# Tail blocks of a fused attention and feed-forward kernel: each batch's 64 query rows on half of TensorE's columns

## The chip, the cores and the metric

The kernel runs on one core of one Trainium2 chip. The metric is device microseconds of one execution. Engine names are those of the profile: PE is TensorE's matmul, PEld its weight load, DVE VectorE, ACT ScalarE, POOL GpSimd, SP the queue that issues most of the DMAs.

## The reference

Causal attention mixed with a retrieved memory, then a gated feed-forward layer. B=4 batches, H=8 heads, S=576 positions, D=64; the feed-forward layer has 512 inputs and 1536 hidden units. Cut to what matters:

```python
scores = scale * q @ k.T ; causal mask ; a = exp(scores - max) ; a /= a.sum(-1) + 1e-9
local = a @ v
q_p = where(q > 0, q, exp(q) - 1) + 1
mem_out = (q_p @ M_prev) / (q_p @ z_prev + 1e-6)
x = g * mem_out + (1 - g) * local          # g = sigmoid(beta), per head
xn = x / rms(x) * rms_g                     # x as 2304 rows of 512
out = (silu(xn @ w_gate) * (xn @ w_val)) @ w_out
```

## The kernel before

**Blocks.** The 2304 rows are worked on in 18 blocks of 128 rows. 576 is four and a half times 128, so each batch has four full blocks and 64 rows over. Two batches share one block for these rows: block 10 holds the last 64 rows of batches 0 and 1, block 17 those of batches 2 and 3. These two are the tail blocks. Rows 0 to 63 of a tail block belong to one batch, rows 64 to 127 to the next. Below they are tail 10 and tail 17.

**Precision.** Operands are split into a high and a low f16 part. Scores are the product of a query tile that holds both parts with a key tile, in two products (`t2` = 0, 1); P V takes three (high by high, high by low, low by high), of 65, 64 and 65 columns; the memory part takes two of 65 columns. The 65th column carries the sum that the result is divided by.

**A tail block before.** TensorE's stationary operand is 128 columns wide, one column for each row of the block. A tail block's keys, values and memory differ between its two halves, so each product is made twice with all 128 rows, once for each batch, into two PSUM tiles, and of each result the half of the rows that doesn't belong to the batch is left unread:

- Scores (`tail_scores`, line 624): for each of 8 heads and each batch four key blocks by two products of 128 columns (L635), evacuated by DVE 64 rows at a time (L639), then two products with the block's own keys (L645, evacuated at L648). 18 products a head.
- P V (`tail_pv`, L748 to L750): for each head, each batch and each of five key blocks three products. 30 a head. The two batches accumulate in the PSUM tiles `a0` and `a1`.
- Memory (`mem_mm`, L848): for each group of four heads and each batch eight products. 32 a block, and two such blocks.

Line 608 and lines 731 to 733 are the scores and P V of full blocks. L848 serves both kinds of block. Between a head's scores and its P V stand the evacuation on DVE, the exponential (ACT, L674), a cast (ACT, L190), the low part (DVE, L693) and a transposing DMA into a `PT` tile (SP, L699).

**The feed-forward layer** works on 9 chunks of two blocks: gate and value products of 256 columns (L1109), then the output products of 512 columns (L1183 to L1185). Its products fill the time in which attention waits. Chunk 8, the last, needs tail 17.

**The order of issue.** `ISSUE` (line 72) writes out for each engine the order of its instructions: letters are kinds (`S` scores, `P` P V, `M` memory, `G` gate and value, `D` output products on PE), a number is a count, and `~` picks one out of turn. Each engine works through its list in that order, so a product that waits holds back all that stand behind it. In the order before, a tail's products mostly alternate with `G` products.

**Buffers.** Scores go through two PSUM buffers (`sc`), which a head of a tail needs three times. `a0` and `a1` have one buffer each.

Of the kernel before, what the change touches and what calls it, by code (L numbers as in the profile page):

```python
# [17 lines left out]
ALU = mybir.AluOpType  # L18
# [66 lines left out]
        "GSD3PDPDPDGPGPGPGPGPSGPSGPSGPSGPSGSGSGSG5PGPGPGPGPGPGPGP5D4SDSDSGSGSGSGSGSPGSPGSPGSPGSPGSPGSPGSPGSPGPGPGPG3S2G5"  # L85
        "D3PDPDPDGPGPGS16PGPGPGPGPGPGPG8PGPGPGPGPGPGPS2GP4YPD4MDMDMGMGMGMGMGMS16GMGMGMGMGMGMGMGMG11D6G2S2G9S8G13D6S6PSPS"
        "P5S2P26GPGPGPGPGPGPGPGPGPGPGPGP2S8GPGPGPGPGPGPGPS8GPGPGPGPGP2S2PD6GPGPGPGPGPGPGPGPS16GPGPGPGPGPGPGPGPGPGPGPGPGP"
        "S2GPGPGP2S8P5~5PP~4PP~3PP~2DPP~1S8P~1PDPDPDPDPDPGPGPGS2PGPGPGPGPGPGPGPGPGPGPGPGPG6SGSGSGS5DSDSDS2DSDSDSM16S2GS"
        "G23D3S8D3G2P20P~10PP~9PP~8PP~7PP~6PP~5PP~4PP~3PP~2PP~1P11GPGPGPSGPSGPSGPSGPSGPSGPSGPSG5PGPGPGPGPGPGPGP5DPDPDPDPD"
        "PDPGPGPGPGPGPSGPSGPSGPSGPSGPSGPSGPSG5PGPGPGPGPGPGPGP5DPDPDPDPDPDPGPGPGPGPGPGPGPGPGPGPGPGPG5SGSGSGSGSGSGSGSD6G12"  # L90
        "M8G5MGMGMGMGMGMGMGMD6G9P24G15D5P12DG4SS~5G13PGPGPGPGPGPGPGP5D6G21S10G3D6G14S6M8S6G10D3MDMDMDMGMGMGMGMGS12G19D5P9"
        "S6DGP9G8SGSGSGSGSGSG8SGSGS6D6G13P9G6S2P9S6G5D6G14P18G3MGMGMGMGMYGMGMGMD3GS8D3G4S2P9S6G12SGSGSGSGSGSGSP9GSD6G17SG"
        "SGSGSGSGSGSGSD6S8G12M6P24M2G9P12G3D6G5SGSGSGSGSGSP12GSGSG12D6P12G24D6G13P12G11P12D6G17S2S2~6G7D4S12D2G2P12G7M8G3"
        "S16G12D6GM4GMGMSGMGMS3G14S4~2GS4G4D6P12D2D2~1S2P12S4D2S6G34MGMGMGMGMGMGMGMP12G7D6G6P12G18D3SDSDSDSGSGSP9G3PGPGPG"
        "PGPGPGPGPGPG4SGSGSGSGSGSG2D4MDMDM6P5G10PGPGPGPG4SGSGSGSGSGSG2D4PDPDPGPGPGPGPGPGPG11SGSGSGSGSGSG2D4PDPDPGPGPGPGPG"
        "PSGPSGSGSGSGSGSGSG5PGPGPGPGPGPGPGP2D4SDSDSGSGSGSGSGSPGPGPGPGPGPGPGPGPG11D3SDSDSDGSGSGSGSGSPGPGPGPGPGPGPGPGPG11D4"
# [12 lines left out]
        "EHCAEHCEACOEOHCEACHNfsXksAECHEFACHEsCsAeEqCHAECHEACHAECHvNfXrAECHkAkHECAFEsHCsAECHECAOoOHEACHE2CE2ACHEvEvAvCsHsq"  # L109
        "AEfNEHCrkAHAXHFs2AqNHfrAEXCECHkEAEFHCEAECHEACsHECs3EACeO2CqHEACov~1v4EHCEACAEHCNfEqCHXrEAC2HEAkHkCAHAFHrAHEkE3C2"  # L110
        "EfNEAqEXEFHCAECErHEACHCEAO2HCNfCAqXkECHAECFHrAECHAECHEACHECAHECANfHXkAECHFAECHEACHEACHEACO2HAECHAECHNEAXCHECAHEC"
        "EACHECAHECAHAHNAXHAHAHAO2HAHAHAHAHAHAHAHAHAHAHO"
    ),
    "DVE": (
        ".2.~1.3I3fIJfZIZfIfI3e~6e~15e~25S4IJe~33UJSiS3iS4TUS4i~1ui2uTi~1u2i~1Tui~2ii~1uTiRiRfRfU2RU6ZUA2tZtUtAt~1tAte~7"
        "t2Ue~15o2fS6fS2i2AuAu2i2~1UA2s2eU2ZTUgege2Ue3AeAe~8UZUAiAg2g~6gg~5gg~4sg2g~2g~4UTg5Ux2AiAsUegxZUS4xeUgeS4eig~16x"
        "eiUe4UuxTuZg~16uUAi~1Ai~1xigZXgg~6Ugg~5TU~1gg~4g2g~2g~4g3Uxgg~1g2g~6gg~5gg~4g2g~2g~4g3Agz~5AgUixUxf2UxAXAkUxqAqA"
        "qvqvqxQkrxUx~3qx~3xqx2~3qkx~4qxAqzAQFxAqAf2rvS2kS2MxM~2AMS2M~1FAMLMLAS2AS2Zv2xALA2zqS2VLAzqVzqVzqzS2QzrzkA2LyS2V"
        "MLAyVMAVMyvALAf2yS2MvVqLMXFVqyMSAVqLvyALqSVyqSAVQvAVyMrL2MySMfAXfAykMqLMqSMqyLAqVSFAqVyQVrALASLSA2SALALV2MVM2SfA"
        "fASLXkSLq3AqAqLMQM2FSArALSV3LA2S2ALALSLA2LVMVMVMSfAfAXSkLSq2AqALq2FQMrM2SALAV3SLA2SLSA2LSLV2AVALM2fMfXSkA2LSFALA"  # L120
        "SM3LSAeAqV2LVSA2LS3A2LS3eqVAeqVAeqVe2qLe2QMSvSe~8fMXrfMASM2ASLkASkAS2LSASAFS2LS2ASALVSV4LSA2M2SMoSM2A2SLSLS2A2L"
# [18 lines left out]
def attn_memory_moe_kernel(  # L140
# [484 lines left out]
    def tail_scores(n, h, s, nm, t, w):  # L625
# [915 lines left out]
```

## Time and profile before

| what | value |
|---|---|
| three runs | 623.01, 628.40, 629.44 us; median 628.4 us |
| the profiled execution | 622.36 us, of which the trace spans 620.6 us |
| PE busy | 598.5 us (96%), 6092 instructions |
| PEld busy | 474.6 us (76%) |
| DVE busy | 451.1 us (73%) |
| ACT busy | 396.8 us (64%) |
| POOL busy | 136.6 us (22%) |
| mean granted TensorE clock | 0.995 |

A product's time in the trace runs from its start to its modelled end, and products overlap: one of 65 columns is shown as 193 ns long, though the next can start about 30 ns later. What a product takes of TensorE's time is therefore read as the distance from its start to the next start in a stretch without waits. The timeline merges neighbours of one kind into a row with a count. Such a row's length is the distances between its starts and one full duration at the end.

### The profile page before, as it was taken

To read this page: it belongs to the slowest core of one execution; us is meant where nothing else is said; L and a number is where in the kernel's file an instruction comes from. 1 tells how busy PE (TensorE), PEld (TensorE's weight loads), DVE (VectorE), ACT (ScalarE), POOL (GpSimd) and SP (SyncE) were. 2 spreads that over 40 slices of the span, in tenths; PEclk is the share of its full clock that TensorE was granted. 3 is DMA by queue.
4 is the path that set the end of the run, shared out by engine and by line. 5 is a ranking of instruction groups with operands and counts; after the bars stand their busy time and mean duration, and the time that the engine had idled before them with its cause. 6 is when DMAs were issued, how large, how long until landed. Compare 5 with 4: busy or idle time off the path is not lost. (4 is left out here: it accounts for less than half of the span.)

```text
span 620.6 us, 15845 instructions
## 1 busy us (share of the span) xinstructions
PE 598.5 (96%) x6092; PEld 474.6 (76%) x6092; DVE 451.1 (73%) x1319; ACT 396.8 (64%) x856; POOL 136.6 (22%) x221
## 2 busy tenths in 40 slices
PE   5979999999999999999999999999999999999996
PEld 4868887677876878788888778778787888887774
DVE  3767688999999687776997777797886757853221
ACT  4587677999887667676466766875775644433221
POOL 2240001124323222121213221132221221112111
PEclk9989999999999999999999999999999999999999
DMA  7997336479868796887489379559995543520001
GB/s 264 361 335 295 103 124 202 135 172 229 149 107 164 149 178 116 176 162 125 71 146 167 80 154 188 106 109 161 164 158 108 86 91 72 94 54 18 35 1 35
DMA packets 183787, 87.57 MB, mean 141 GB/s; under 512 B 165792, under 2 KB 165792, under 8 KB 183712
## 3 DMA queue, kind: packets, MB, share of 16 engines
q1 hardware_dynamic: 180640, 81.82, 62.0%
q10 hardware_dynamic: 3072, 4.74, 2.3%
q8 instruction: 48, 0.79, 0.5%
q14 instruction: 27, 0.22, 0.1%
HBM read 37.77 MB, written 4.72 MB: 68 GB/s over the span
## 5 line engine op out<-in xcount | busy, mean ns | idle before, releaser
L1109 PE MATMUL gv<-xT,wgv 128*128 128x256 f16 x2304 | 312.6, 273 | 0.7 <-DMA xT<-x 0.5
L1109 PEld LDWEIGHTS <-wgv 128*128 128x128 f16 x2304 | 220.0, 98 | 38.9 <-issue 1.5
L1148 POOL TENSOR_TENSOR h<-th,h 128x256 f16<-128x256 f32 x88 | 65.8, 748 | 291.1 <-ACT h L1147 283.8
L674 ACT ACTIVATE S<-S,nm 128x256 f32<-128x256 f32 (+3 forms) x112 | 70.8, 639 | 41.0 <-DVE nm L614 28.4
L1127 DVE SCALAR_TENSOR_TENSOR th<-th,gv 128x256 f32<-128x256 f32 x96 | 39.9, 415 | 62.0 <-ACT th L1126 61.7
L608 PE MATMUL sc<-kT,qT 128*128 128x128 f16 x576 | 79.3, 220 | 0.8 <-DVE nm L614 0.5
L693 DVE SCALAR_TENSOR_TENSOR P<-S,P 128x512 f16<-128x512 f32 (+2 forms) x96 | 67.4, 703 | 17.4 <-ACT P L190 16.8
L1126 ACT ACTIVATE th<-gv,wt 128x256 f32<-128x256 f32 x96 | 44.5, 463 | 54.3 <-PE gv L1109 50.1
L614 DVE CUSTOM_DVE_ANT_0 S<-sc,mask,qsc 128x256 f32<-128x256 f32 (+2 forms) x96 | 57.4, 610 | 17.2 <-PE sc L608 16.7
L1184 PE MATMUL out<-wo,h 128*128 128x512 f16 x176 | 66.8, 380 | 0.0
L1183 PE MATMUL out<-wo,h 128*128 128x512 f16 x176 | 66.3, 379 | 0.0
L1185 PE MATMUL out<-wo,h 128*128 128x512 f16 x176 | 66.1, 379 | 0.0
L190 ACT ACTIVATE P<-S 128x512 f16<-128x512 f32 (+2 forms) x96 | 58.0, 605 | 12.7 <-DMA PT<-P 10.7
L1147 ACT CAST h<-th 128x256 f16<-128x256 f32 x88 | 35.1, 399 | 46.5 <-DVE th L1130 39.0
L608 PEld LDWEIGHTS <-qT 128*128 128x128 f16 x576 | 48.3, 98 | 7.3 <-issue 1.8
L1102 PE MATMUL gv<-xT,wgv 128*128 128x256 f32 x192 | 46.9, 395 | 0.8 <-DVE xT L919 0.8
L1130 DVE SCALAR_TENSOR_TENSOR th<-th,wt,gv 128x256 f32<-128x256 f32 x96 | 45.8, 477 | 1.8
L1102 PEld LDWEIGHTS gv<-xT,wgv 128*128 128x128 f32 x192 | 36.6, 197 | 7.7 <-issue 1.9
L731 PE MATMUL loc<-v,PT 128*128 128x65 f16 x288 | 40.9, 193 | 1.0 <-DMA PT<-P 1.0
L733 PE MATMUL loc<-v,PT 128*128 128x65 f16 x288 | 41.2, 193 | 0.0
L732 PE MATMUL loc<-v,PT 128*128 128x64 f16 x288 | 40.6, 194 | 0.0
L1185 PEld LDWEIGHTS <-h 128*128 128x128 f16 x176 | 17.1, 98 | 19.5
(231 smaller groups left out, 1133.5 us busy)
## 6 DMA issues: line engine op xcount, KB each, us to landing
kv<-in_qkv_dram SPq DMA_DIRECT2D x40, 256.0 KB, 3.6
q<-in_qkv_dram SPq DMA_DIRECT2D x18, 256.0 KB, 3.5
wo<-in_moe_w_out_dram SPq DMA_DIRECT2D x8, 512.0 KB, 3.9
out_dram<-res ACTq DMA_DIRECT2D x16, 256.0 KB, 3.2
wgv<-in_moe_w_val_dram SPq DMA_DIRECT2D x7, 512.0 KB, 7.7
wo<-in_moe_w_gate_dram SPq DMA_DIRECT2D x7, 512.0 KB, 9.1
qT<-qT SPq DMA_DIRECT2D x28, 128.0 KB, 3.5
wgv<-in_moe_w_gate_dram SPq DMA_DIRECT2D x5, 512.0 KB, 6.2
```

The source lines that it names most:

```text
L190: got = fn(*p, **k)
L608: nc.tensor.matmul(t[:, g * w + j * P : g * w + (j + 1) * P], qT[n][:, t2, h, :], kT[blk_of[(b, j)]][:, h, :], start=(t2 == 0), stop=(t2 = ...
L614: nc.vector.tensor_tensor_reduce(out=s[:, g * w : (g + 1) * w], in0=t[:, g * w : (g + 1) * w], in1=mask[:, m0 : m0 + w], scale=qsc[n][:, 5 ...
L674: nc.scalar.activation(v_, v_, AF.Exp, bias=nm[:, g : g + 1], scale=-1.0)
L693: m = nc.vector.scalar_tensor_tensor(out=p16[:, w : 2 * w], in0=s[:, :w], scalar=PSCALE, in1=p16[:, :w], op0=ALU.mult, op1=ALU.subtract)
L1102: nc.tensor.matmul(o, wgv[:, 1 + p, o0 : o0 + P], xT[0][:, cc, :], start=(cc == 0), stop=(cc == NC - 1))
L1109: nc.tensor.matmul(o, lhs, xT[c][:, rhs, :], start=(cnt == 0), stop=(cnt == 3 * NC - 1))
L1130: nc.vector.scalar_tensor_tensor(out=th, in0=th, scalar=sc_h, in1=gvp[F][:, 1, :], op0=ALU.mult, op1=ALU.mult)
L1148: nc.gpsimd.tensor_tensor(h16[:, 1], th, h16[:, 0], ALU.subtract)
L1183: nc.tensor.matmul(o, hh, whi, start=(f == 0), stop=False)
L1184: nc.tensor.matmul(o, hh, wlo, start=False, stop=False)
L1185: nc.tensor.matmul(o, hl, whi, start=False, stop=(f == NF - 1))
```

## The change

A tail's two batches now go to different halves of TensorE's columns. For each product the stationary operand is a 64 column slice of the query (or P, or phi) tile, and the result goes to rows 0 to 63 or 64 to 127 of one PSUM tile. The products for the two halves stand next to each other in the order. Counted over the built program, 832 products that were 128 columns wide (288 scores, 480 P V, 64 memory) become 864 that are 64 wide: 320, 480 and 64, which is 432 pairs. Since both halves land in one tile, the evacuations on DVE treat 128 rows at once, `sc` is needed twice a head, and P V and memory of a tail use `a0` for the first four heads and `a1` for the others, as full blocks do. The second memory group is issued before the first P V of the block, as in full blocks. `ISSUE` is written anew from the first tail on, with all of a head's scores in a row (`S20`) and all of its P V (`P30`). The clearing of `mask` moves to the front of the DVE list. `m_proj` gets arguments that nobody passes.

```diff
     def tail_scores(n, h, s, nm, t, w):
...
-        for bb in range(2):
-            r = slice(bb * TR, bb * TR + TR)
-            if bb:
-                t = ps.tile([P, 512], F32, tag="sc", name="sc")
-            for j in range(NI):
-                for t2 in range(2):
+        for j in range(NI):
+            for t2 in range(2):
+                for bb, r in enumerate(HALVES):
                     nc.tensor.matmul(
-                        t[:, j * P : (j + 1) * P], qT[n][:, t2, h, :],
+                        t[r, j * P : (j + 1) * P], qT[n][:, t2, h, r],
                         kT[blk_of[(b + bb, j)]][:, h, :], start=(t2 == 0), stop=(t2 == 1),
                     )
...
         for t2 in range(2):
-            nc.tensor.matmul(
-                t[:, :P], qT[n][:, t2, h, :], kT[n][:, h, :], start=(t2 == 0), stop=(t2 == 1)
-            )
+            for r in HALVES:
+                nc.tensor.matmul(
+                    t[r, :P], qT[n][:, t2, h, r], kT[n][:, h, :], start=(t2 == 0), stop=(t2 == 1)
+                )
...
     def tail_pv(n, h, pt):
...
+            for bb, r in enumerate(HALVES):
+                nc.tensor.matmul(a[r], pt[:, j, r], vt[bb][:, h, : D + 1], start=(j == 0), stop=False)
+            for bb, r in enumerate(HALVES):
+                nc.tensor.matmul(a[r, :D], pt[:, j, r], vt[bb][:, h, D + 2 :], start=False, stop=False)
+            for bb, r in enumerate(HALVES):
+                nc.tensor.matmul(a[r], pt[:, nb + j, r], vt[bb][:, h, : D + 1], start=False, stop=(j == nb - 1))
...
     def mem_mm(n, g4):
...
+                for bb, r in enumerate([slice(0, P)] if i < NI else HALVES):
                     nc.tensor.matmul(
-                        acc[:, hh, :], phT[n][:, h, :], M16[b + bb][:, t2, h, : D + 1],
+                        acc[r, hh, :], phT[n][:, h, r], M16[b + bb][:, t2, h, : D + 1],
```

What it moves is seen in the order. On PE, in the middle of the first head of tail 10 before, a score product (L635, `kT` the keys, 128 rows by 128 columns) alternates with a gate product of the feed-forward layer (L1109):

```order
L635 LDWEIGHTS qT_4005
L635 MATMUL sc<-kT_1882,qT_4005 128x128
L1109 LDWEIGHTS wgv
L1109 MATMUL gv_4196<-xT_2983,wgv 128x256
L635 LDWEIGHTS qT_4005
L635 MATMUL sc<-kT_3070,qT_4005 128x128
```

In the changed kernel the same head's scores (now L627, 64 rows by 128 columns) begin behind a gate product (now L1086):

```order
L1086 LDWEIGHTS wgv
L1086 MATMUL gv_4196<-xT_2983,wgv 128x256
L627 LDWEIGHTS qT_4005
L627 MATMUL sc<-kT_1331,qT_4005 64x128
L627 LDWEIGHTS qT_4005
L627 MATMUL sc<-kT_1353,qT_4005 64x128
L627 LDWEIGHTS qT_4005
L627 MATMUL sc<-kT_1331,qT_4005 64x128
```

The head's 20 score products now stand in a row, the keys of the two batches (`kT_1331`, `kT_1353`) in turn, with no gate product among them. Over both tails the 864 products stand in 26 such stretches, so PE goes over from whole-array to half-array products and back 52 times in all.

On DVE the same head's evacuation before is two of 64 rows by 512 columns (L639) and one of the block's own keys (L648); the `ISA nm` rows read the row maximum out:

```order
L639 ISA S,nm<-sc,mask,qsc 64x512
L639 ISA nm 64x1
L639 ISA S,nm<-sc,mask,qsc 64x512
L639 ISA nm 64x1
L648 ISA S,nm<-sct,tmask,nm,qsc 128x128
L648 ISA nm 128x1
```

In the changed kernel the same place on DVE (now L631 and L641):

```order
L631 ISA S,nm<-sc,mask,qsc 128x512
L631 ISA nm 128x1
L641 ISA S,nm<-sct,tmask,nm,qsc 128x128
L641 ISA nm 128x1
```

One evacuation of 512 columns a head is gone, 16 over both tails.

## Rows read from the trace of the kernel before

**Rows 1.** Busy time by stretch: stretch, length, PE, PEld, DVE, ACT, POOL, clock, DMA, GB/s.

```profile
285.00:350.00 65.00, 64.56 (x846) 53.25 (x844) 51.97 (x146) 37.76 (x73) 15.50 (x26) 1.00 0.68 121
505.00:560.00 55.00, 55.00 (x760) 45.89 (x758) 38.13 (x105) 23.10 (x42) 10.11 (x16) 1.00 0.37 73
```

**Rows 2.** Groups of instructions: shapes and count, busy us, mean ns, idle before.

```profile
L848 PE MATMUL mem<-M,phT 128*128 128x65 f16 x256 | 27.9, 193 | 0.0
L635 PE MATMUL sc<-kT,qT 128*128 128x128 f16 x256 | 24.8, 219 | 0.2 <-DVE nm L639 0.2
L639 DVE CUSTOM_DVE_ANT_0 S<-sc,mask,qsc 64x512 f32<-64x512 f32 x32 | 23.9, 747 | 5.2 <-PE sc L635 4.7
L748 PE MATMUL loc<-v,PT 128*128 128x65 f16 x160 | 23.8, 193 | 0.0
```

**Rows 3.** Timeline of PE in the tails: start us, length us, instruction, count, idle before.

```profile
311.02 0.27 PE L645 MATMUL sct<-kT,qT 128*128 128x128 f16 x2 [0.20 <-DVE nm L639]
311.13 0.19 PE L749 MATMUL loc<-v,PT 128*128 128x64 f16 x1
...
311.89 0.19 PE L750 MATMUL loc<-v,PT 128*128 128x65 f16 x1
...
313.97 0.61 PE L635 MATMUL sc<-kT,qT 128*128 128x128 f16 x8 [0.19 <-DVE nm L639]
...
549.22 0.65 PE L848 MATMUL mem<-M,phT 128*128 128x65 f16 x16
```

**Rows 4.** Timeline of PE: products on all 128 rows and on 64 (csum<-kv).

```profile
77.41 0.68 PE L277 MATMUL csum<-pre 128*128 128x128 bf16 x9
...
84.42 0.39 PE L277 MATMUL csum<-pre 128*128 128x128 bf16 x4
84.75 0.40 PE L277 MATMUL csum<-kv 64*128 64x128 bf16 x4
85.08 0.41 PE L277 MATMUL csum<-wgv 128*128 128x128 bf16 x4
```

**Rows 5.** Timeline of PE: f32 scores of full blocks, contracted over 64 rows.

```profile
51.27 1.16 PE L597 MATMUL sc<-k,q 64*128 64x128 f32 x16 [0.66 <-ACT q L533]
...
89.86 1.16 PE L597 MATMUL sc<-k,q 64*128 64x128 f32 x8
```

**Rows 6.** Weight loads by line, min/median/max ns, and a stretch of the timeline.

```profile
L258 PEld LDWEIGHTS allp<-ident,wmx x8: 79/81/83, 73.7 to 148.9; 128*2 128x2 f32 x6, 128*1 128x1 f32 x2
L811 PEld LDWEIGHTS loc<-kv,PT x64: 186/192/223, 23.9 to 109.9; 128*128 128x128 f32 x64
L811 PE MATMUL loc<-kv,PT x64: 218/275/323, 24.1 to 109.9; 128*128 128x64 f32 x64
83.76 0.83 PE L811 MATMUL loc<-kv,PT 128*128 128x64 f32 x6
```

**Rows 7.** From tail 17's last scores to its `PT` tile: timeline of DVE; DMA issues.

```profile
547.61 0.41 DVE L648 CUSTOM_DVE_ANT_0 S<-sct,tmask,nm 128x128 f32<-128x128 f32 x1
549.69 0.82 DVE L693 SCALAR_TENSOR_TENSOR P<-S,P 128x640 f16<-128x640 f32 x1 [1.67 <-ACT P L190]
PT<-P SPq DMA_TRANSPOSE x11, 3.4
```

**Rows 8.** After tail 17: timeline of PE; the DMA of chunk 8's input.

```profile
558.13 2.78 PE L1109 MATMUL gv<-xT,wgv 128*128 128x256 f16 x24
562.04 2.78 PE L1109 MATMUL gv<-xT,wgv 128*128 128x256 f16 x24
L934 SPq DMA_TRANSPOSE xT<-x x1: 1232/1232/1232, 563.6 to 563.6; - x1
DMA to landing us min/median/max: 3.0/3.0/3.0
```

**Rows 9.** Timeline of the start.

```profile
1.06 0.27 DVE L292 MEMSET mask<- 128x256 uint32 x1
6.18 1.09 PE L531 MATMUL tp<-ident,kv 128*128 128x128 f32 x4 [6.18 <-DMA kv<-in_qkv_dram]
```

More of the change, by code (lines that the diff above doesn't have):

```diff
@@ L279, in gram @@
                 after(m, event[ev])
+    mask = const.tile([P, NI * P], BF16, name="mask")
+    nc.vector.memset(mask, 0.0)
     ident = const.tile([P, P], F32, name="ident")
@@ L290, in attn_memory_moe_kernel @@
     nc.vector.memset(mhalf[:, 1:2], 1.0)
-    mask = const.tile([P, NI * P], BF16, name="mask")
-    nc.vector.memset(mask, 0.0)
     nc.gpsimd.affine_select(
@@ L739, in tail_pv @@
         nb = NI + 1
[L740 to L750 removed]
+        if hh == 0:
+            accs[n, g4] = ps.tile([P, 4, D + 1], F32, tag=f"a{g4}", name=f"loc{n}_{g4}", bufs=1)
+        a = accs[n, g4][:, hh, :]
+        for j in range(nb):
+            vt = [v16[n if j == NI else blk_of[(b + bb, j)]] for bb in range(2)]
+            for bb, r in enumerate(HALVES):
[4 more added lines that the diff above has]
+                nc.tensor.matmul(a[r], pt[:, nb + j, r], vt[bb][:, h, : D + 1], start=False, stop=(j == nb - 1))
     t1s = {}
@@ L867, in loc_evac @@
             return evac32(n, g4)
-        i = blocks[n][1]
-        if i < NI:
-            parts = [(slice(0, P), accs.pop((n, g4)))]
-        else:
-            parts = [(slice(bb * TR, bb * TR + TR), accs.pop((n, g4, bb))) for bb in range(2)]
+        acc = accs.pop((n, g4))
         if g4 == 0:
@@ L876, in loc_evac @@
         f = tiny.tile([P, 4], F32, tag="fm", name="fl", bufs=3)
-        for r, acc in parts:
-            tot, gain = acc[r, :, D], consts_of(n)[r, 8 + H + 4 * g4 : 12 + H + 4 * g4]
-            nc.vector.scalar_tensor_tensor(
-                out=f[r], in0=tot, scalar=1e-9 * PSCALE, in1=gain, op0=ALU.add, op1=ALU.mult
-            )
-        nc.vector.reciprocal(f, f)
-        for r, acc in parts:
-            rows = r.stop - r.start
-            nc.vector.tensor_tensor(
-                t2[r, four(n, g4), :], acc[r, :, :D],
-                f[r].unsqueeze(2).to_broadcast([rows, 4, D]), ALU.mult,
-            )
+        gain = consts_of(n)[:, 8 + H + 4 * g4 : 12 + H + 4 * g4]
+        nc.vector.scalar_tensor_tensor(
+            out=f, in0=acc[:, :, D], scalar=1e-9 * PSCALE, in1=gain, op0=ALU.add, op1=ALU.mult
+        )
+        nc.vector.reciprocal(f, f)
+        nc.vector.tensor_tensor(
+            t2[:, four(n, g4), :], acc[:, :, :D], f.unsqueeze(2).to_broadcast([P, 4, D]), ALU.mult,
+        )
         nc.gpsimd.tensor_tensor(
@@ L1091, in m_proj @@
     @keep("G")
-    def m_proj(F, m):
+    def m_proj(F, m, part=0, parts=1):
         c, f = F // NF, F % NF
-        if m == 0:
+        if m == 0 and part == 0:
             gvp[F] = ps.tile([P, 2, 2 * P], F32, tag="gv", name=f"gv{F}")
-        o = gvp[F][:, m, :]
+        at = slice(part * 2 * P // parts, (part + 1) * 2 * P // parts)
+        o = gvp[F][:, m, at]
         cnt = 0
@@ L1345, in attn_memory_moe_kernel @@
                 a(1, 0.6, mem_mm, 1, 0)
-            if hp == max(0, 4 - max(G, 2)) and not is_tail[np_]:
+            if hp == max(0, 4 - max(G, 2)):
                 a(np_, 0.6, mem_mm, np_, 1)
```

122 lines of the change are left out of this document (47 added, 75 removed).

## The prediction

> **What bounds the kernel now.** I read the busy times by stretch first, since the shares of the page mix stages. In both stretches in which the tails run, 285 to 350 us and 505 to 560 us, PE is busy all the time (64.56 of 65.00 us and 55.00 of 55.00) at a clock of 1.00, which is the level of 2.4 GHz, while DVE is idle for 20 and 31% of the time and ACT and POOL for more [rows 1]. Then the groups: the tail's products have next to no idle time before them [rows 2]. So TensorE's stream of products sets the time here, and what the change takes from or adds to that stream goes into the end of the program nearly in full. Busy time itself says nothing about the price of a product, since products overlap; I price them by the distance between starts in the timeline.
>
> **Before, the tails' share of that stream.** Eight scores of 128 columns take 0.61 us, of which the last keeps its full 0.219 [rows 2, 3]: (0.61 - 0.22) / 7 = 56 ns each. From 311.13 to 311.89 us there are 25 distances between P V products, 0.76 / 25 = 30 ns each; 16 memory products take (0.65 - 0.19) / 15 = 31 ns each [rows 2, 3]. Every one has a weight load of 128 f16 columns of its own, so such a load hides behind a product of 30 ns. The counts are 288 scores, 480 P V, 64 memory:
> 288 x 0.056 + 480 x 0.030 + 64 x 0.031 = 16.1 + 14.4 + 2.0 = 32.5 us.
>
> **After, the pairs.** There are 432 pairs, 160 of scores and 272 of P V and memory. Two questions set the price of a pair, and the trace answers neither directly, since no product on half of the columns runs in it.
>
> Do the halves overlap? The nearest rows are products on half of the array's rows. 16 of them on alternating halves take 1.16 us, as do 8 on one half alone [rows 5]. So halves of rows run side by side, weight loads included, and a pair costs what one product costs. I take the same for columns.
>
> How fast are the loads? Loads of f32 are the slow kind in this trace: 2 columns take 81 ns, 128 take 192 [rows 6], so a column costs 111 / 126 = 0.88 ns, and products of 64 columns behind them are held to (0.83 - 0.275) / 5 = 111 ns apart [rows 6]. Whole f16 loads take less than a third of that, as the 30 ns show. A load of 64 columns is then bounded by 30 ns, if it keeps the speed of the whole f16 load or better, and 56 ns, if it goes at the f32 speed (64 x 0.88). I take 56: the f32 load is the nearest case in this trace of one that doesn't get the fast treatment, and half a load is another shape than the fast one.
> The Trainium skill speaks for that end: in "TensorEngine Tiling (Array Packing)", Restrictions and Gotchas, column tiling excludes the fast weight load, and "TensorE: Matmul & The Clock Gate", LDWEIGHTS, gives columns / 1.2 ns for a plain load, which as an estimate is 53 ns for 64 columns. By that the sum below would be 0.8 us lower; no run here shows it yet.
>
> With 56 ns for a load, a pair of scores costs 56 ns (its columns and its loads need the same), and a pair of P V or memory also 56, set by the loads instead of 30 by the columns. 432 x 0.056 = 24.2 us. That is a gain of 8.3 us, all of it in the scores (16.1 to 9.0, 7.1 us) and the rest small: P V and memory go from 16.4 to 15.2.
>
> **The switches.** Where products on 64 rows follow such on 128, four of them and the way to the next kind take 84.75 - 84.42 = 0.33 us, and the same back, 85.08 - 84.75 = 0.33; four distances without a switch are 4 x (0.68 - 0.22) / 8 = 0.23 [rows 4]. A switch costs 0.10 us. The new order has 52: +5.2 us. From below this could be 0, if columns need no switch; from above 0.16 (0.33 - 3 x 0.058, should the product ahead hide nothing), 8.3 us. I take 0.10, by the nearest row. Before, the tails had no switch.
>
> **Waits that go.** At 311.02 and 313.97 us PE waits 0.20 and 0.19 us for DVE to free a score buffer [rows 3], which a head needed three times and now twice. -0.4 us.
>
> **Work off the path.** DVE loses 16 evacuations of 747 ns [rows 2], 12 us, and the doubled small operations of memory and P V. DVE has idle time in both tails [rows 1], so this is worth nothing but the 0.4 above. The clearing of `mask`, 0.27 us, now precedes `ident` on DVE, but PE's first product needs a DMA that comes at 6.18 us [rows 9]: nothing. Without that cover it would cost 0.27.
> New waits: PE no longer has gate products between a head's products, so a late `PT` tile stalls the whole block. The tightest is the last head of tail 17. Between its scores and its P V now stand 60 pairs (3.4 us), 24 gate and 12 output products. A gate product takes (2.78 - 0.27) / 23 = 0.109 us, and 562.04 - 558.13 holds 24 of them and 6 output products, which gives 0.216 for one of these [rows 8]; together 3.4 + 2.6 + 2.6 = 8.6 us. The chain there: from the evacuation of the own keys at 547.61 to the end of the low part at 550.51 is 2.9, the `PT` transfer 3.4 [rows 7], the evacuation of 512 columns 0.75 ahead of it [rows 2]: 7.1 us. It is covered by 1.5 us. After the last P V stand 72 gate and 18 output products of chunk 7 (11.7 us) where there were 48 and 18 (9.1), against some 8.5 us up to the landing of chunk 8's input (558.13 to 563.6, + 3.0) [rows 8]: nothing.
>
> **The sum**, against the profiled execution's 622.4 us: -8.3 + 5.2 - 0.4 = -3.5, so 618.9. That execution is 6.0 us under the median of the three runs, 628.4; I carry the difference onto the median, 624.9 us, 0.6% faster. No change is reached at a pair price of (32.5 - 5.2 + 0.4) / 432 = 64 ns, just above the 56 taken.
>
> **The rivals.**
> *Loads keep up.* A half load takes 30 ns or less. Then pairs of scores cost 56 and the other 272 cost 30: 9.0 + 8.2 = 17.2, a gain of 15.3, in all -10.5: 617.9 us. For it: whole f16 loads hide behind 30 ns. Against: the half has another shape than the load that is fast.
> *Loads of the two halves come one after the other.* The halves of rows, which overlap, feed on different partitions; the halves of columns read the same 128 partitions. If their weights pass one door, a pair costs two loads, 112 ns, and nothing of the streaming matters: 432 x 0.112 = 48.4, +15.9 + 5.2 - 0.4 = +20.7: 649.1 us, slower. It decides from 64 ns a pair on. For it: the shared partitions. Against: the rows of halves.
> The Trainium skill has a rule to this end in "TensorE: Matmul & The Clock Gate", Part 3, What overlaps and what doesn't: loads overlap running products only when the row group differs, which two column halves don't. The trace speaks against it in whole-array products, whose loads hide behind products of the same rows [rows 3]; for halves no run shows it yet.
> *The halves take turns.* The change then doesn't do what it says: 320 scores at 56 and 544 others at 30 are 34.2 us, +1.7 + 5.2 - 0.4 = +6.5: 634.9 us. Against it stand rows 5 alone.
>
> **How the numbers follow.** Forecast 0.50, loads keep up 0.22, one door 0.11, turns 0.12, and 0.05 for something else, such as waits in the new blocks. A measurement of this kernel tells changes from about 1% on, 6.3 us (its own runs lie 1% apart). Faster by more: nearly all of the loads that keep up and a sixth of the forecast's case (no price for a switch), 0.28. Slower by more: one door, half of the turns and part of the rest, 0.20. Within 1%: 0.52. The range reaches from the loads that keep up, and a little below since the runs scatter, 615, to the turns, 636; it leaves out one door and a part of the others.
>
> **What would show it.** Distances between starts in the new score blocks: pairs 56 ns apart confirm the halves side by side, 112 refutes it. In the P V blocks: pairs 56 ns apart are slow loads, 30 fast ones, 112 one door. Load durations of 64 columns near 81 + 56 = 137 ns against 97 for a whole one. 0.10 us at the borders of the 26 blocks. No idle PE before the last P V. The prediction is wrong if a pair lies off 56 by more than 10 ns, or if the new blocks wait.

## The result and the profile after

The changed kernel takes 625.6 us (median of 20 runs) against 623.2 us of the kernel before (20 runs). The ratio is 1.0062, with a 95% interval from 1.0045 to 1.0079: it is slower by 0.6%, where 0.6% faster was forecast. The runs of each kernel fall into two groups some 8 us apart: the medians are taken over all twenty, the ratio over the lower group of each (medians 625.4 and 621.4 us). The profiled execution took 625.1 us, its trace spans 623.4 us, and the mean granted clock is 0.989. The first gate product of the feed-forward layer starts somewhere between 34.0 and 45.1 us in the profiles, whatever the kernel (34.6 and 45.0 us in the two profiles of the changed kernel), so below traces are compared by stretches behind that point, not by their spans.

First the page of the changed kernel: busy time and count, then PE's busy share and the granted clock in 40 slices.

```profile
span 623.4 us, 15863 instructions
PE 590.9 (95%) x6124; PEld 458.6 (74%) x6124; DVE 433.0 (69%) x1271; ACT 396.4 (64%) x856; POOL 132.9 (21%) x221
PE   5789999999999999999998999999999999989996
PEclk9979999999999999999999989999999999989999
```

PE is busy 7.6 us less than before and the program is longer. The missing nines behind the start stand where the tails are. The two stretches of [rows 1], now in the changed kernel:

```profile
285.00:350.00 65.00, 61.26 (x861) 45.68 (x858) 43.51 (x124) 37.05 (x72) 12.66 (x27) 1.00 0.60 112
505.00:560.00 55.00, 52.31 (x791) 39.83 (x789) 29.59 (x83) 24.45 (x46) 11.57 (x18) 0.97 0.43 79
```

PE now idles 3.7 and 2.7 us there, where it idled 0.4 and 0.

**The products themselves** came out better than forecast. The timeline of PE in tail 17: start, length, line, count of one head's scores and of a P V block behind them.

```profile
543.73 0.49 PE L1086 MATMUL gv<-xT,wgv 128*128 128x256 f16 x3
544.15 0.64 PE L627 MATMUL sc<-kT,qT 128*64 128x128 f16 x16
544.62 0.28 PE L638 MATMUL sct<-kT,qT 128*64 128x128 f16 x4
544.73 0.20 PE L739 MATMUL loc<-v,PT 128*64 128x65 f16 x2
544.76 0.20 PE L741 MATMUL loc<-v,PT 128*64 128x64 f16 x2
544.79 0.20 PE L743 MATMUL loc<-v,PT 128*64 128x65 f16 x2
...
545.17 0.20 PE L743 MATMUL loc<-v,PT 128*64 128x65 f16 x2
545.30 0.39 PE L1160 MATMUL out<-wo,h 128*128 128x512 f16 x1
```

Eight pairs of scores take 544.62 - 544.15 = 0.47 us, 59 ns a pair (the first pair of a block is slower). Fifteen pairs of P V span 545.17 - 544.73 = 0.44 us over 14 distances, 31 ns a pair; in other blocks 31 to 35. So both halves together take what one whole product takes in [rows 3]. The switch stands at both ends: the last gate product starts at 543.73 + 0.49 - 0.27 = 543.95, and the next thing 0.20 us later, where gate products are 0.11 apart; behind the block 0.13 where P V products are 0.03 apart. That is 0.09 and 0.10 us. The weight loads, by shape (busy us, mean ns):

```profile
L604 PEld LDWEIGHTS <-qT 128*128 128x128 f16 x576 | 48.2, 98 | 11.2 <-issue 6.9 <-DMA qT<-qT 0.4
L627 PEld LDWEIGHTS <-qT 128*64 128x64 f16 x256 | 7.6, 110 | 2.6 <-issue 2.1
L739 PEld LDWEIGHTS <-PT 128*64 128x64 f16 x160 | 8.2, 113 | 5.0 <-DMA PT<-P 3.0 <-issue 1.9
```

Half a load lasts 110 to 113 ns and a whole one 98, but a load's length is not its price: two of the longer ones go with each pair, and the pairs start 31 ns apart.

Summed over the 26 blocks, from the first start to the last in each, the tails' products take 20.4 us, of which 2.9 is one wait. That leaves 17.5 us. The last pair of each block begins there and its own price stands behind it, 13 times 56 ns and 13 times 30 ns, 1.1 us in all: 18.6 us against 32.5, a gain of 13.9. Of these 18.6 us, 0.3 is a slow clock behind the wait (last section), so the products by themselves gain 14.2.

**The waits** ate it. PE's four longest waits in the changed kernel behind the start of the program: what waited, for what, us in total, times, longest.

```profile
PE loc L739 <- DMA PT<-P: 2.7, 1, 2.7
PE sc L604 <- DMA kT<-row: 2.0, 1, 2.0
PE loc L724 <- DVE t L844: 1.9, 1, 1.9
PE sc L604 <- DVE nm L631: 1.7, 1, 1.7
```

Only the first is in a tail's own block. L604 and L724 are the scores and P V of full blocks, those behind tail 10. To place such losses I cut each trace at the same gate and value products of the feed-forward layer (2496 of them in every kernel), counted in order of start, and take the distance between their starts. The waits are the distances on PE that exceed a product's own streaming by more than 0.16 us, in the first stretch (behind a wait they can hold a few distances of 0.2 us that are a slow clock's):

```
stretch (gate products)      931 to 1656   1656 to 1931   1931 to 2281   2281 to end   waits in the first
                             (tail 10)                    (tail 17)
before                       161.0         53.2           76.6           42.9           3.3
changed kernel, profile 1    167.1         53.2           75.9           42.9          12.3
changed kernel, profile 2    165.8         53.2           75.8           42.9          11.9
```

The loss stands around tail 10 and the blocks behind it, +6.1 and +4.8 us. Tail 17 gains 0.7, of the 5 that its products should give (half of 14.2 less 22 switches of 0.095).

### The profile page after: what moved, and what is told of

It reads as the page before. It is cut to its first block, busy times and chain, and to the rows that moved or that the text cites. A ratio compares the mean times of both kernels' runs of the same rounds, so it can differ in the third digit from the quotient of the medians.

```text
span 623.4 us, 15863 instructions
## 1 busy us (share of the span) xinstructions
PE 590.9 (95%) x6124; PEld 458.6 (74%) x6124; DVE 433.0 (69%) x1271; ACT 396.4 (64%) x856; POOL 132.9 (21%) x221
## 5 line engine op out<-in xcount | busy, mean ns | idle before, releaser
L1086 PE MATMUL gv<-xT,wgv 128*128 128x256 f16 x2304 | 306.1, 274 | 1.9 <-DMA xT<-x 1.6
L1086 PEld LDWEIGHTS <-wgv 128*128 128x128 f16 x2304 | 220.7, 98 | 44.8 <-issue 3.5
L1125 POOL TENSOR_TENSOR h<-th,h 128x256 f16<-128x256 f32 x88 | 64.2, 729 | 287.6 <-ACT h L1124 283.5
L667 ACT ACTIVATE S<-S,nm 128x256 f32<-128x256 f32 (+3 forms) x112 | 70.5, 640 | 51.4 <-DVE nm L610 32.3
L686 DVE SCALAR_TENSOR_TENSOR P<-S,P 128x512 f16<-128x512 f32 (+2 forms) x96 | 67.4, 704 | 31.0 <-ACT P L184 30.7
L604 PE MATMUL sc<-kT,qT 128*128 128x128 f16 x576 | 78.1, 219 | 5.4 <-DMA kT<-row 2.0
L604 PEld LDWEIGHTS <-qT 128*128 128x128 f16 x576 | 48.2, 98 | 11.2 <-issue 6.9
L724 PE MATMUL loc<-v,PT 128*128 128x65 f16 x288 | 41.1, 193 | 3.9 <-DVE t L844 1.9
L725 PE MATMUL loc<-v,PT 128*128 128x64 f16 x288 | 40.8, 194 | 0.0
L724 PEld LDWEIGHTS <-PT 128*128 128x128 f16 x288 | 27.4, 97 | 8.4 <-DMA PT<-P 3.1
```

Of the source, the lines that this page charges most:

```text
L604: nc.tensor.matmul(t[:, g * w + j * P : g * w + (j + 1) * P], qT[n][:, t2, h, :], kT[blk_of[(b, j)]][:, h, :], start=(t2 == 0), stop=(t2 = ...
L667: nc.scalar.activation(v_, v_, AF.Exp, bias=nm[:, g : g + 1], scale=-1.0)
L686: m = nc.vector.scalar_tensor_tensor(out=p16[:, w : 2 * w], in0=s[:, :w], scalar=PSCALE, in1=p16[:, :w], op0=ALU.mult, op1=ALU.subtract)
L724: nc.tensor.matmul(a, phi_, vhi, start=(j == 0), stop=False)
L1086: nc.tensor.matmul(o, lhs, xT[c][:, rhs, :], start=(cnt == 0), stop=(cnt == 3 * NC - 1))
L1125: nc.gpsimd.tensor_tensor(h16[:, 1], th, h16[:, 0], ALU.subtract)
```

## The experiments

The edits of the order are shown as they stand in the list of the engine named. Two theories were set against each other from the start. A: the waits are made by places of the rewritten order. B: behind a faster TensorE the other engines set the end, whatever the order. What each run did to the two tails' stretches, cut as above, with one profile for each row:

```
run                tail 10 (931 to 1656)   tail 17 (1931 to 2281)   waits in the first
keep_first         157.9                   72.6                      3.9
keep_last          164.2                   72.7                     10.3
turns              169.3                   75.9                     10.0
less               162.3                   74.4                      8.8
old_17             166.3                   72.6                     12.4
old_10             160.5                   75.6                      6.6
scatter            171.1                   82.0                      3.4
nudge              166.8                   72.1                     11.7
s_first_p_last     163.7                   72.5                      9.2
only_scores        160.5                   74.8                      4.0
nudge_sp           169.9                   72.0                     14.3
nudge_p            168.3                   71.9                     12.2
best               158.5                   72.0                      4.5
pe_new_rest_old    168.6                   74.2                     13.0
best_again         159.0                   72.0                      5.1
```

How far a single profile can be trusted shows where an order comes more than once. Up to the end of the first stretch keep_first, best, best_again and old_10 have the same order, and it took 157.9, 158.5, 159.0 and 160.5 us; the changed kernel's order (two profiles and old_17) took 167.1, 165.8 and 166.3. So the two orders lie 5 to 9 us apart, and a difference of some 2.5 us between two single profiles of this stretch can be chance. Tail 17's stretch repeats within 0.4 us.

**keep_last and keep_first: the new products in the old order.** PE's list, end of tail 17's part, before and in keep_first (what stood mixed now stands in blocks; 62 switches in keep_last and 60 in keep_first, 52 in the changed kernel):

```diff
-PGPGPGPGPGPGS11PSGPSGPSGPSGPSGPGPGP3D6G4S2G20D2M16D4G24D6
+P30D3G17S20G7D6G24D2M16D4G24D6
```

A head's products, scattered before, are moved together to the place of the last or of the first of them; all else stays.

> The changed kernel's products on the two column halves, but in the order of issue of the kernel before on every engine (its order of the memory parts too); each tail head's 20 score, 30 P V or 16 memory products stand together where the last of them stood. Theory A (the gain of the products, some 15 us less the 5 us of the switches, is lost to waits that the rewritten order makes: products ahead of their data): the waits go, and it is about 10 us faster than the kernel before, ratio 0.98 to 0.99. Theory B (behind a faster TensorE the scores' evictions, exponentials, casts and transfers set the end of this stretch, whatever the order): the waits come back at other places, ratio 0.995 to 1.008.

Measured: 0.998 (0.994 to 1.002).

> As the one before, but each head's products stand together where the first of them stood. They come earlier on TensorE, so P V products can wait for their transposed probabilities. Theory A: still faster than the kernel before, 0.98 to 0.995, less than with the last place if those waits appear. Theory B: 0.995 to 1.01.

Measured: 0.9927 (0.989 to 0.997), 616.6 us against 621.9, faster than both kernels. PE's waits in it, as above:

```profile
PE sc L604 <- DVE nm L610: 1.7, 4, 0.6
PE loc L724 <- DMA PT<-P: 1.1, 2, 0.7
```

and the two stretches of time of [rows 1]:

```profile
285.00:350.00 65.00, 64.36 (x921) 48.65 (x919) 46.44 (x133) 41.69 (x83) 13.54 (x27) 1.00 0.69 129
505.00:560.00 55.00, 55.00 (x815) 41.32 (x814) 30.50 (x85) 25.71 (x47) 10.95 (x18) 1.00 0.42 78
```

PE is as busy as before. In tail 17 both kernels of this pair give what the rows say: half of -14.2, and 30 switches at 0.095 us, is about -4.2, and the stretch is 4.0 and 3.9 us shorter. Around tail 10 only keep_first gains, 3.1 us, and its order repeated gains 0.5 to 2.6 against the one profile of before. So the order costs the changed kernel its gain, and within one order the place of a block decides as well. keep_first lies in theory A's range; keep_last lies in B's, but its tail 17 gains as A says, so B, which holds whatever the order, falls as it stood. The direction of the place was expected the other way: earlier is better here.

**turns: the halves one after the other.** The loop over the halves moves outside the loops over keys, in scores, P V and memory:

```diff
-            for bb, r in enumerate(HALVES):
-                nc.tensor.matmul(a[r], pt[:, j, r], vt[bb][:, h, : D + 1], start=(j == 0), stop=False)
...
+        for bb, r in enumerate(HALVES):
+            for j in range(nb):
+                vt = v16[n if j == NI else blk_of[(b + bb, j)]]
+                nc.tensor.matmul(a[r], pt[:, j, r], vt[:, h, : D + 1], start=(j == 0), stop=False)
...
```

> The changed kernel in its own order, but in each tail head all products of one half stand ahead of all of the other, so that the halves hardly run side by side. A product of the scores then takes at least its 56 ns and one of P V at least its 29 ns by itself: the blocks take at least 16 us more of TensorE (160 x 56 ns + 272 x 29 ns = 16.8). Theory A (the waits hang on single places of the order, TensorE paces the rest): most of it shows, the end 10 to 17 us later than the changed kernel's, ratio to the kernel before 1.022 to 1.033. Theory B (the other engines pace the tails' stretch): the present waits of some 15 us take it up, the end at most 5 us later, ratio 1.005 to 1.014.

Measured: 1.0116 (1.007 to 1.016). PE in a P V block of it:

```profile
326.60 0.22 PE L739 MATMUL loc<-v,PT 128*64 128x65 f16 x1
326.66 0.20 PE L740 MATMUL loc<-v,PT 128*64 128x64 f16 x1
326.69 0.20 PE L741 MATMUL loc<-v,PT 128*64 128x65 f16 x1
```

One half product now takes 31 ns by itself, as two side by side did. The blocks take 26.0 us, 8.5 more than the 17.5. At least 16 more were expected: scores take 41 ns a product on average, since only part of a head's scores stand alone, 56 ns apart, and the others still start beside one of the other half (distances of 6 and 50 ns, or 30 and 26). Of these 8.5 tail 17 shows nothing, since its 2.9 us wait goes and with it a slow clock behind it (below), and tail 10 shows 2.2 to 3.5. So in the changed order much of what TensorE's products cost or save is taken up by waits. The ratio lies in theory B's range, but both ranges were worked out from 16 us, so it doesn't decide between them.

**less: fewer products in the same order.** The P V products of P's high part with V's low part are left out in the tails, 80 pairs.

```diff
-            for bb, r in enumerate(HALVES):
-                nc.tensor.matmul(a[r, :D], pt[:, j, r], vt[bb][:, h, D + 2 :], start=False, stop=False)
```

> The changed kernel without the P V products with the low part of V in the two tail blocks (144 pairs by 8 heads' 5 blocks of keys, in all 80 pairs per block of rows group: 160 products of 80 pairs in two tails; at 33 ns a pair some 2.6 us of TensorE). This leaves out that part of the computation. Theory A: the end moves with TensorE, 2 to 3 us earlier than the changed kernel's, ratio to the kernel before 1.001 to 1.003. Theory B: the time saved turns into waits, the end within 1 us of the changed kernel's, ratio 1.005 to 1.008.

Measured: 0.9954 (0.990 to 1.001). In tail 17 the 1.3 us of 40 pairs show as 1.4 to 1.5. Around tail 10 it is 3.5 to 4.8 us, more than the products are worth: waits there come and go with small shifts. It is faster than either theory said.

**after_again, old_17, old_10: which stretch.** The changed kernel once more, and its order joined with that of keep_first between blocks 14 and 17, where on every engine both lists have issued the same set.

> The changed kernel once more, beside the next three on the same chip. All theories: 1.0045 to 1.008 of the kernel before.

Measured: 1.0034 (0.999 to 1.008), a little under what was expected, with the first ratio, 1.0062, inside its interval.

```diff
-S20P30D6G24D6P120G24D6
+S20G7D6G24D2M16D4G24D6P120G24D6
```

> The changed kernel with its own order up to block 14, and from there (tail block 17) the order of the kernel before, each head's products where the first of them stood. Where the loss against keep_first (0.9927 beside 1.0062, 8.4 us) comes from the order, it can be split by place. Theory A1 (it lies mostly in the order around tail 10, and the 2.85 us wait ahead of the last four heads of tail 17 is the smaller share): about 2.9 us earlier than the changed kernel, ratio 1.000 to 1.003. Rival A2 (the end of the program counts most, since nothing behind it can make up for a wait): 5 us or more earlier, ratio 0.994 to 0.998.

Measured: 1.0016 (0.998 to 1.006). The stretch of tail 17 comes to 72.6 us, the other stays. The edit of old_10 is the mirror of this one, in tail 10's part.

> The other half: the order of the kernel before up to block 14 (each head's products where the first of them stood), and the changed kernel's own order for tail 17. Theory A1: 5 to 6 us earlier than the changed kernel, ratio 0.996 to 0.999. Rival A2: at most 3.5 us earlier, 1.000 to 1.003.

Measured: 0.9944 (0.991 to 0.998). The stretch of tail 10 comes to 160.5. The two halves of the loss are separate, and the larger one is around tail 10, as A1 says; the ratio is lower still than A1's 0.996 to 0.999.

**scatter: not kept together.** As keep_first, with P V pair by pair between gate products:

```diff
-G10P30G7P30G5S20
+G10P12GP2G2P2G2P2G2P2G2P2G2P2GP2GP2GP2GP2GS20
```

> As keep_first, but the pairs of P V stand where those products stood before, one pair at a time between gate and output products: 266 changes between half and whole products instead of 60. If each change costs TensorE the 0.095 us that the changed kernel's rows show, it is 206 x 0.095 = 19.6 us later than keep_first less the 4 us of waits that keep_first has there, ratio 1.017 to 1.026. Rival (the price is hidden where a pair only fills a gap, or the drain is that of the block's first load alone): at most 6 us later, ratio 0.993 to 1.003.

Measured: 1.0315 (1.025 to 1.038), above the expected range. Against keep_first both stretches together are 22.5 us longer, 22.5 / 206 = 0.109 us for each added switch (0.10 against old_10's 160.5 around tail 10), though PE waits no more than there. The price of a switch is paid in full; keeping products together is what makes the change worth doing at all.

**nudge: three waits taken out of the changed kernel by hand.** First PE's list. Then DVE's at two places, where `S` is an eviction of scores (L631 and L641 of tail 10's head 7), `L` a low part (L686), `M` three steps of a memory eviction (L842 to L844), `r` and `k` casts (L213), `V` an eviction of P V (L858 to L862).

```diff
-D6G24D6P120G24D6
+D6G24D6G24P120D6
```

```diff
-MSMASALV3A2S2LA2S4
+MSMASASLSV3A2LA2S4
...
-S2AqAq2fqfqQLrMkMAMAV2
+S2AqAMqMqMfqfqQLrkA2V2
```

> The changed kernel with three of its waits taken out by hand, each by moving what is waited for ahead in its engine's order: VectorE evicts the scores of tail 10's last head ahead of head 6's low part (the 1.91 us wait of block 11's scores), VectorE evicts a memory part ahead of a low part and two casts (the 2.10 us wait of P V behind it), and TensorE does one more gate step of 24 products ahead of the last four heads of tail 17 (the 2.85 us wait). Read by stretch, from gate product to gate product. Theory A (places of the new order make the waits, each by itself): the stretch around tail 10, 167.1 and 165.8 us in two profiles of the changed kernel, comes to 162 to 163.5, that of tail 17 (75.9) to 73.1 to 73.4, ratio 0.994 to 0.999. Theory B (what is behind those engines is late anyway, so a wait taken out comes back at the next place): less than half of it, over 164.5 and over 74.7, ratio 0.999 to 1.005.

Measured: 0.9984 (0.994 to 1.003). Tail 17 did more than expected, 75.9 to 72.1 us; around tail 10 nothing moved, 166.8. What PE waits for in it:

```profile
PE sc L604 <- DMA kT<-row: 2.5, 1, 2.5
PE sc L604 <- DVE nm L610: 2.4, 4, 1.2
PE sc L604 <- DMA qT<-qT: 1.8, 2, 1.5
PE sc L604 <- DMA qT<-row: 1.8, 1, 1.8
```

The waits for L631 and L844 are gone, the one for the transposed keys of block 11 has grown, and two for transposed queries have come up. So A holds for tail 17, and for tail 10 something like B: with this order the preparation of the blocks behind it is late as well, and a wait removed comes back at the next of its results.

**s_first_p_last: scores early, P V late**, otherwise keep_first:

```diff
-S20G13D6P60G12S20G12D6GP30G7S20
+S20G13D6P30G12S20G12P30D6G8S20
```

> As keep_first, but the P V products of each head stand where the last of them stood, the scores and memory parts where the first stood. It tells what made keep_last slower around tail 10 (164.2 us against 157.9). If late scores (each head's chain of eviction, exponential, cast, low part and transfer starts later, and the kernels' score buffers come free later): like keep_first, 158 to 160 us, ratio 0.990 to 0.996. If late P V (the accumulators come free later for what follows): like keep_last, 163 to 165 us, ratio 0.996 to 1.001.

Measured: 0.997 (0.993 to 1.001), and 163.7 us around tail 10, as keep_last's 164.2 and above the 157.9 to 160.5 of scores and P V early. By these profiles it is P V that must not be late. How it spreads begins in DVE's timeline, of this run and then of keep_first:

```profile
326.59 0.16 DVE L858 SCALAR_TENSOR_TENSOR fl<-loc,tcb 128x4 f32<-128x4 f32 x1 [1.92 <-PE loc L743]
327.34 0.81 DVE L686 SCALAR_TENSOR_TENSOR P<-S,P 128x640 f16<-128x640 f32 x1
```

```profile
329.90 0.16 DVE L858 SCALAR_TENSOR_TENSOR fl<-loc,tcb 128x4 f32<-128x4 f32 x1
331.64 0.83 DVE L686 SCALAR_TENSOR_TENSOR P<-S,P 128x640 f16<-128x640 f32 x1 [0.92 <-ACT P L184]
```

With P V late, DVE stands 1.92 us before it can evict the first four heads. The low part behind it in DVE's list starts 40.6 us into the stretch instead of 38.7, the transfer of block 11's keys 40.8 instead of 38.9, that of the low part's head 42.1 instead of 40.3, and block 11's first scores 46.5 instead of 44.6. That all of this goes through DVE is not shown: the ACT instruction that the low part needs ends late in this run as well (40.3 instead of 38.7), behind a wait of its own for a transfer:

```profile
326.37 0.74 ACT L184 ACTIVATE P<-S 128x640 f16<-128x640 f32 x1 [0.83 <-DMA PT<-P]
```

**only_scores: one part alone.** The kernel before with the tails' scores on halves, 20 in a row, and nothing else.

```diff
-S16PGPGPGPGPGPGPG8PGPGPGPGPGPGPS2GP4
+S20PGPGPGPGPGPGPG8PGPGPGPGPGPGPGP4
```

> The kernel before with only the tails' scores on the two halves, each head's 20 products where the first of them stood; P V and memory parts as before. By the rows a head's scores take 0.585 us for 10 pairs instead of 18 x 56 ns = 1.01, and two changes of 0.095 us: 0.23 us gained a head, 1.9 us a tail. Theory A (in before's order the products' price reaches the end): the stretch of tail 17 comes to 74.5 to 75.0 us (before 76.6, keep_first 72.6), that of tail 10 to 159 to 161, ratio 0.993 to 0.998. If the whole gain of keep_first lies in P V and the memory parts: 76.3 to 76.9, ratio 0.998 to 1.002.

Measured: 1.003 (0.999 to 1.0075), outside of what was expected for the end. By stretch it is as expected, 74.8 and 160.5 us, 1.8 and 0.5 shorter than before, and from the 931st gate product to the end its profile is 2.3 us shorter (331.5 against 333.8). The ratio doesn't show these 0.4%, and its interval just excludes them. It takes in the start, which the stretches leave out: this profile's first gate product stands at 44.9 us, 7.3 later than before's, and its run is counted in the ratio. How much of the difference comes from it is not shown. The 1.8 us of tail 17 are clear of the scatter, the 0.5 are not.

**nudge_sp and nudge_p: is it one place of SP's queue, or P V's own?** In SP's list the transfer of block 11's keys (`k`) goes ahead of that of phi (`F`'s), and in nudge_p besides the last three heads' P V go ahead of scores and gate products in PE's list:

```diff
-XrLr2kLblLFlbLkL3
+XrLr2kLblLkFlbL4
```

```diff
-D6G5S~6GS~6G3S8GSGSGP30SGSG11D6G5
+D6G5P30S~6GS~6G3S8GSGSGSGSG9P30G2D6G5
```

> As nudge, and on SyncE's queue the transfer that transposes block 11's keys stands ahead of the phi transfer, as in the kernel before (it started 44.1 us behind the stretch's first gate product in nudge, 38.9 in keep_first). If the place in that queue is what block 11's scores wait for (2.65 us, and what is late behind them): the wait goes, and the stretch around tail 10 comes from 166.8 to 162.5 to 164.5 us. If the time comes back once more at the next place: over 165.5 us.

Measured: 1.0095 (1.001 to 1.018), 169.9 us, 3.1 more than nudge: not shorter. SP's queue in nudge and then in nudge_sp, where the stretch's first gate product comes 7.1 us later (295.0 us against 287.8):

```profile
324.50 1.26 SPq L477 DMA_TRANSPOSE phT<-row  x1
325.82 0.57 SPq L338 DMA_DIRECT2D kv<-in_qkv_dram  x1
...
331.91 1.78 SPq L477 DMA_TRANSPOSE kT<-row  x1
```

```profile
335.14 1.23 SPq L477 DMA_TRANSPOSE kT<-row  x1
336.46 1.45 SPq L477 DMA_TRANSPOSE phT<-row  x1
337.97 1.17 SPq L338 DMA_DIRECT2D kv<-in_qkv_dram  x1
```

The keys come 3.9 us earlier in the stretch (40.2 instead of 44.1 us into it), but they could not start where they now stand, and hold back a load of keys and values by 5.0 us (43.0 instead of 38.0). ACT needs that load, and PE needs what stands behind it on ACT:

```profile
341.82 0.63 ACT L387 ACTIVATE junk<-kv 128x512 bf16<-128x512 f32 x1 [5.50 <-DMA kv<-in_qkv_dram]
...
342.74 0.68 ACT L1137 ACTIVATE res<-out,wos 128x512 f32<-128x512 f32 x1
```

```profile
343.47 0.59 PE L1160 MATMUL out<-wo,h 128*128 128x512 f16 x1 [3.94 <-ACT res L1137]
```

> As nudge_sp, and on TensorE the P V products of tail 10's last three heads stand ahead of some of block 11's scores and gate products, 3 to 8 us earlier, near where keep_first has them. If late P V, which holds the buffers of the transposed probabilities, paces the blocks behind the tail: 159 to 162.5 us, near keep_first's 157.9. If not: within 1 us of nudge_sp.

Measured: 1.007 (0.995 to 1.018), 168.3 us, not near 159 to 162.5. It is no test of late P V, though: the same wait of PE stands ahead of these products, and they start as late as in nudge (51.4, 56.4 and 61.7 us into the stretch, there 51.3, 57.0 and 61.9).

**pe_new_rest_old: PE's new list with the other engines' old ones.**

> TensorE's order of the changed kernel, with the order of the kernel before on ScalarE, VectorE, GpSimd and SyncE. If the lists of those four engines are what is worse in the changed kernel: the stretch around tail 10 at 162 us or below (keep_first 157.9, changed kernel 166 to 167). If TensorE's own list is (its places of the scores and P V among the gate products): 165 us or more, since the other engines then wait for products that come in another order than theirs; over 168 if the lists no longer fit each other.

The edit is the four lists of ScalarE, VectorE, GpSimd and SyncE, and with them the place in the program at which a tail's second memory part is listed, as it was before; PE's own order is the changed kernel's. Measured: 1.0084 (1.003 to 1.014), 168.6 us. The old lists of the four engines don't cure it. Since it comes to over 168, the lists may not fit each other, and PE's list alone isn't convicted by this run.

**best and best_again: the better order of each stretch**, keep_first's up to block 14 and nudge's for tail 17.

> The order of keep_first up to block 14, and for tail 17 the changed kernel's order with the one gate step moved ahead of the last four heads, as in nudge: the shorter one of each stretch (157.9 and 72.05 us). Sum from the first of these gate products to the end: 326.2 us against 333.8 before and 338 to 339 in the changed kernel, ratio to the kernel before 0.987 to 0.994. Rival (the stretches are not independent, or keep_first's 157.9 was a lucky profile): 0.995 to 1.000.

Measured: 0.994 (0.987 to 1.001), with medians of 617.0 us in six runs against 623.1 in eleven.

> The run named best once more, for its ratio: 0.990 to 0.997 if its order keeps what the profile showed, 0.998 or more if that was chance.

Measured: no ratio; its six runs have a median of 623.2 us, against 622.3 of the kernel before beside it. So its times don't confirm best, and what was asked stays open. By stretch its profile does repeat best: 159.0 and 72.0 us, from the 931st gate product to the end 327.2 against 326.6, and 333.8 before. It is no better than keep_first (326.8), whose interval lies below 1.

## Why the prediction was wrong

**What failed is the step "New waits: none"**, which priced the new order at nothing. It looked at two places, the last head of tail 17 and the input of chunk 8, and the waits in blocks behind a tail were not looked for; in the rivals "something else, such as waits in the new blocks" had 0.05. The budget of the changed kernel behind the 931st gate product: products -14.2, 52 switches of 0.095 us +4.9, waits around tail 10 from 3.3 to 12.3, of which 0.6 is the slow clock's, and in tail 17 from 0 to 2.9, together +11.3, and +3.3 for a slower clock behind two of the waits (last section). That is +5.3 us; this profile shows 339.2 against 333.8, +5.4. The second shows 337.8, +4.0; in it the clock falls behind one wait alone, the one in tail 17.

That the forecast of 624.9 us lies 0.7 from the measured 625.6 is luck. It is a change of -3.5 us carried onto a median of three runs, 628.4, where twenty runs of the kernel before give 623.2; the change itself went the other way.

*In tail 17* the step was worked out as a chain of 7.1 us under a cover of 8.6, and both were off. The chain of [rows 7] in the changed kernel, on DVE, and the DMA's times to landing (min, median, max) for tail 17's last three transfers:

```profile
545.45 0.83 DVE L686 SCALAR_TENSOR_TENSOR P<-S,P 128x640 f16<-128x640 f32 x1 [1.70 <-ACT P L184]
546.19 0.75 DVE L631 CUSTOM_DVE_ANT_0 S<-sc,mask,qsc 128x512 f32<-128x512 f32 x1
...
549.06 0.83 DVE L686 SCALAR_TENSOR_TENSOR P<-S,P 128x640 f16<-128x640 f32 x1 [0.55 <-ACT P L184]
```

```profile
DMA to landing us min/median/max: 3.4/3.6/4.9
```

```profile
554.93 0.26 PE L739 MATMUL loc<-v,PT 128*64 128x65 f16 x2 [2.69 <-DMA PT<-P]
555.00 0.25 PE L741 MATMUL loc<-v,PT 128*64 128x64 f16 x2
```

The last of the last head's scores starts at about 544.7, and its P V at 554.93: 10.2 us, where the chain was put at 7.1. The eviction begins 1.5 us after the scores, since DVE has the low part of the head before in front of it and that waits for ACT; and the transfer takes 4.9 us where [rows 7] has 3.4. The cover was put at 8.6 with pairs of 56 ns; at 31 ns it is shorter by 1.5. One gate step of 24 products more ahead of these heads (nudge) removes the wait, and the stretch comes out 4.5 us under the one before, where half of the products' gain and 22 switches are 5.0 and 0.4 of a wait is left. So this part is shown.

*Around tail 10* the order is shown to be the cause (the same products in the old order take 157.9 to 160.5 us in four profiles, in the new one 165.8 to 167.1 in three), and within the old order the late place of P V alone is worth 3.2 to 5.8 us. Which place of the new order starts it is not shown: each one that was taken away came back at another. The order is a fit of five lists to each other, and a wait of PE is the last link of a chain through them, as the rows of nudge_sp show it link by link for one wait.

**The pair price was mis-sized, in favour.** 56 ns for scores is right. For P V and memory it is 31 to 35 instead of 56: the half load keeps pace with the columns, which is the rival "loads keep up", and 272 x 0.023 = 6.3 us more gain. Taking the f32 load as the nearest case was the wrong row; the whole f16 load, hidden behind 30 ns, was the nearer one. The loads' forecast duration, 137 ns, was 110 to 115. The Trainium skill ("TensorE: Matmul & The Clock Gate", LDWEIGHTS) gives columns / 1.2 ns for a weight load, as an estimate 53 ns for 64 columns; pairs 31 ns apart with two such loads each speak against it as a spacing. The same page's rule that loads overlap running products only where the row group differs (Part 3, What overlaps and what doesn't) doesn't hold here: the halves share all rows, and neither 112 ns a pair nor turns were seen.

**The switch was right**, 0.10 against 0.09 to 0.10 at the borders of the blocks, and 0.10 to 0.11 in scatter over 206 of them.

**Waits that go, and work off the path:** the 0.4 us is too small to be seen, and of DVE's 18 us less (451.1 to 433.0) nothing shows in the time, as said.

With the right pair price, the sum would have been -14.2 + 5.2 - 0.4 = -9.4 us, further from the result than the forecast was. The rival that came true in the products and the failed step pulled in opposite directions, and the step decided.

## What to carry to other kernels

When an engine gets faster in one stretch, price the new order, not only the new instructions: the chain behind each moved group must be followed through every queue it shares, up to the blocks that come after. Keep the order that fits and put the faster instructions into it, then move single places and look at the same stretch of the trace each time; here this gained 0.7% where the rewritten order lost 0.6%. Halves of the columns are worth their place only in blocks, as going over to them and back costs about 0.2 us.

## What the hardware showed that was not expected

Two half-column products start 3 to 4 ns apart and take the time of one: 56 ns a pair of 128 columns, 31 to 35 of 65, with two loads of 110 to 115 ns each for every pair.

A wait of 2 us can cost more than itself. Busy time and granted clock (the column behind POOL) in the changed kernel, before and behind the wait that ends at 359.6 us, and behind the one that ends at 554.9 us:

```profile
357.40:359.40 2.00, 0.29 (x2) 0.00 (x0) 2.00 (x6) 0.35 (x1) 0.02 (x1) 1.00 0.65 125
359.60:361.60 2.00, 1.97 (x17) 0.95 (x18) 1.31 (x5) 0.78 (x2) 0.67 (x1) 0.63 1.03 197
361.60:363.60 2.00, 2.00 (x11) 1.40 (x10) 0.86 (x2) 1.02 (x2) 0.76 (x1) 0.52 1.09 101
```

```profile
554.90:556.90 2.00, 1.97 (x35) 1.63 (x36) 0.77 (x3) 0.00 (x0) 0.00 (x0) 0.50 0.00 0
556.90:558.90 2.00, 2.00 (x15) 1.57 (x13) 0.00 (x0) 0.72 (x2) 1.05 (x3) 0.70 0.00 0
```

PE had stood still for 1.9 and 2.7 us, and afterwards the granted clock was 0.50 to 0.70 in these rows, at the lower level of 1.2 GHz or partly at it, and it was back at 1.00 behind them. That loses (0.37 + 0.48) x 2 = 1.7 us and (0.50 + 0.30) x 2 = 1.6 us. Waits of 1.75 and 1.98 us for L604, which end at 328.1 and 334.4 us, were not followed by such a fall: the clock is 1.00 in the rows behind them. Behind the 2.4 us wait in tail 17 of the second profile it was 0.58 and 0.56 for 2 us each, and behind nudge_sp's 3.9 us wait 0.50 for 4 us.
